# Down-projection pieces in the idle row groups of score phases, and shifted keys copied chunk by chunk

## Chip, cores, metric

One core of one Trainium2 chip runs the whole program. The metric is device time in microseconds, where smaller is better; most runs of one kernel agree within 0.1%. Kernels sent together ran on one chip, with runs of the kernel before in between.

## The reference, cut to what matters

A layer norm feeds two branches. One is attention with 32 heads of 16 channels that share one key and one value head. The other is a SiLU network of width 1792. All inputs are bf16, 2048 rows of 512.

```python
xn = layernorm(x)
s = attention(xn, wq, wk, wv, wo)     # 32 heads, Dh = 16, one k and one v for all
h = silu(xn @ w1)                     # (2048, 1792)
g = silu(h @ w2)                      # the "down projection"
return x + s * g
```

## The kernel before

The program is written by a planner that runs on the host: it simulates the five engines with fixed durations and, whenever an engine is free, places its next operation. What the chip gets is a fixed order for each engine and the semaphore waits between them. Four kinds of TensorE work alternate. A **score phase** computes three or four score tiles of 128 keys by 512 queries at once. Each tile has a contraction of only 32 rows (16 of them hold a head's channels), so it takes one of the array's four row groups and one bank of PSUM, the memory that TensorE writes its results to.

```python
def s_mm(pe, b, g, i, kt):     # tile of head group g, row group i, key block kt
    return pe.matmul(bank(b), lhsT=kt_sb[32 * i:32 * i + 32, g % 2, kt * P:(kt + 1) * P],
                     rhs=qt_sb[32 * i:32 * i + 32, (g // 2) % NQR, :],
                     start=True, stop=True, tile_position=(32 * i, 0))
```

A **column round** is four matmuls with all 128 contraction rows, each making 32 output rows of one bank. The value products are such rounds, and so are the rounds of the projection jobs. A down-projection job has 14 of them; the planner keeps one such job open at a time.

```python
def col4(h, b, lhs, rhs, start, stop, n=NQ):
    for j in range(4):
        last = h.matmul(bank(b)[32 * j:32 * (j + 1), 0:n], lhsT=lhs(j), rhs=rhs, start=start, stop=stop,
                        tile_position=(0, 32 * j), skip_group_check=True)
    return last
...
# mk_z, round ft of 14:
col4(pe, b, lambda j: u_sb[:, ft, r * P + 32 * j:r * P + 32 * (j + 1)], w2_sb[:, ft, :], ft == 0, ft == NFT - 1)
```

The exponential of a score tile is done in one of two ways: by ScalarE (one value product each), or by VectorE as an integer trick with three shifted copies made on GpSimd (four value products each). The odd head groups need the keys shifted down by 16 rows. These were zero-filled early and copied by four DMAs once all keys existed:

```python
pl.add(Task(PO, 1800.0, lambda g: g.memset(kt_sb[:, 1, :], 0.0), (), [("kt1", i) for i in range(4)], 3, ...))
...
def add_kt1():                 # called when the last of four key chunks is done
    for i in range(4):
        kt1[i] = pl.add(Task(SP, 60.0, lambda e, i=i: e.dma_start(
            kt_sb[32 * i + DH:32 * i + 32, 1, :], kt_sb[32 * i:32 * i + DH, 0, :]), ...
```

Thresholds in the planner are varied at random from a seed.

The softmax here doesn't subtract the row's maximum and nothing guards it: scores larger than these inputs give would overflow.

## Time and profile before

| | before |
|---|---|
| time, median of 4 (range) | 679.01 us (677.96 to 679.11) |
| profiled span | 677.3 us |
| busy: TensorE, ScalarE, VectorE, GpSimd | 98, 97, 90, 83% |
| score tiles, of these on VectorE | 2048, 732 |
| score phases of three and of four tiles | 536, 110 |
| column rounds of down-projection jobs | 224 |

A group line of the profile reads: source line, engine, operation, output and inputs by name, shapes, count, then busy time in us and mean ns of one, then the engine's idle time just before. The phases and rounds were counted by sorting TensorE's records in time. The lines themselves are in the prediction.

### The profile page before, as it was taken

How to read it: one execution, taken by the hardware profiler on the slowest of the kernel's cores; microseconds unless marked ns; L12 is line 12 of the kernel's file. 1: busy time of each engine (PE TensorE's matmuls, PEld its weight loads, DVE VectorE, ACT ScalarE, POOL GpSimd, SP SyncE). 2: the span in 40 equal slices, each digit the busy share in tenths (PEclk: the TensorE clock that was granted, in tenths of full speed). 3: DMA queues.
4: the chain of work that ended last, by engine and by line, in shares of the span. 5: the costliest groups of instructions: out<-in, count | busy, mean ns of one | idle time of the engine just before them, and what ended most of it. 6: DMA issues, size and time to landing. Idle time of an engine off the chain costs nothing.

```text
span 677.3 us, 21172 instructions
## 1 busy us (share of the span) xinstructions
PE 663.9 (98%) x8941; PEld 192.1 (28%) x8941; DVE 610.0 (90%) x1081; ACT 655.1 (97%) x763; POOL 564.9 (83%) x561
## 2 busy tenths in 40 slices
PE   7899999999999999999999999999999999999997
PEld 4322222222222222222222222222222222222233
DVE  8979998989889999998899999988989999998873
ACT  6899999999999999999999999999999999999995
POOL 3049888999998899899899889889989988998992
PEclk9989999999999999999999999999999999999999
DMA  8410000000000000000000010000000001000000
GB/s 302 137 18 1 3 2 2 2 2 2 2 2 17 19 17 17 2 2 2 2 1 2 3 33 17 18 2 1 2 2 2 2 1 33 18 18 2 2 1 33
DMA packets 11437, 12.66 MB, mean 19 GB/s; under 512 B 1808, under 2 KB 10768, under 8 KB 11344
## 3 DMA queue, kind: packets, MB, share of 16 engines
q1 hardware_dynamic: 11056, 11.05, 5.1%
q8 instruction: 72, 1.18, 0.7%
q10 hardware_dynamic: 288, 0.26, 0.1%
q14 instruction: 21, 0.17, 0.1%
HBM read 8.95 MB, written 2.10 MB: 16 GB/s over the span
## 4 chain that ended last, share of the span: by engine, by line
PE 76%; ACT 12%; DVE 9%; issue 1%; DMA 0%; ACTq 0%
PE ps L1177 32%; PE ps L847 26%; PE ps L503 18%; ACT pa_sb L1518 11%; DVE db_sb L1039 3%; DVE stats_sb L450 1%; DVE u_sb L652 1%; ACT t_sb L650 1%; DVE xn_sb L479 0%; DVE xnT_sb L530 0%; DVE f_sb L1224 0%; DMA ds_sb<-in_A_x_dram 0%; DVE fin_sb L702 0%; DVE otr_sb L1228 0%; DVE kt_sb L559 0%
## 5 line engine op out<-in xcount | busy, mean ns | idle before, releaser
L1106 POOL INT64_ADD ds_sb<-db_sb x549 | 559.2, 1040 | 98.5 <-DVE db_sb L1039 43.1
L1518 ACT ACTIVATE pa_sb<-ps 128x1024 bf16<-128x1024 f32 (+2 forms) x674 | 621.4, 1019 | 8.9 <-PE ps L847 7.9
L1039 DVE TENSOR_SCALAR db_sb<-ps 128x512 uint16<-128x512 f32 x732 | 474.9, 683 | 47.3 <-PE ps L847 40.6
L1177 PE MATMUL ps<-ds_sb,v_sb 128*32 128x512 bf16 x2196 | 274.9, 383 | 0.0
L847 PE MATMUL ps<-qt_sb,kt_sb 32*128 32x512 bf16 x2048 | 253.5, 385 | 5.9 <-ACT pa_sb L1518 1.8
L1177 PE MATMUL ps<-pa_sb,v_sb 128*32 128x512 bf16 x1316 | 243.7, 384 | 0.0
L1177 PE MATMUL ps<-db_sb,v_sb 128*32 128x512 bf16 x732 | 178.4, 384 | 0.6 <-DVE f_sb L1224 0.6
L847 PEld LDWEIGHTS ps<-qt_sb,kt_sb 32*128 32x128 bf16 x2048 | 63.1, 91 | 281.3 <-ACT pa_sb L1518 155.7
L1177 PEld LDWEIGHTS ps<-ds_sb,v_sb 128*32 128x32 bf16 x2196 | 68.5, 95 | 60.0 <-issue 41.2
L503 PE MATMUL ps<-xnT_sb,w_sb 128*32 128x512 bf16 x896 | 72.9, 386 | 0.0
L1177 PEld LDWEIGHTS ps<-pa_sb,v_sb 128*32 128x32 bf16 x1316 | 60.0, 95 | 38.9 <-issue 27.4
L503 PE MATMUL ps<-w_sb,u_sb 128*32 128x512 bf16 x896 | 70.7, 384 | 0.0
L1177 PEld LDWEIGHTS ps<-db_sb,v_sb 128*32 128x32 bf16 x732 | 43.8, 95 | 18.3 <-issue 12.5
L650 ACT ACTIVATE t_sb<-ps 128x512 bf16<-128x512 f32 x72 | 44.1, 613 | 0.0
L652 DVE SCALAR_TENSOR_TENSOR u_sb<-t_sb,ps 128x512 bf16<-128x512 bf16 x56 | 38.3, 684 | 0.8
L503 PEld LDWEIGHTS ps<-w_sb,u_sb 128*32 128x32 bf16 x896 | 17.2, 94 | 27.2 <-issue 23.1
L503 PEld LDWEIGHTS ps<-xnT_sb,w_sb 128*32 128x32 bf16 x896 | 16.7, 94 | 27.4 <-issue 22.0
L1224 DVE STREAM_TRANSPOSE f_sb<-ps 128x512 f32<-128x512 f32 x31 | 21.9, 706 | 0.0
L652 DVE SCALAR_TENSOR_TENSOR tmp_sb<-t_sb,ps 128x512 bf16<-128x512 bf16 x16 | 11.0, 685 | 10.0 <-ACT t_sb L650 9.6
L503 PE MATMUL ps<-xnT_sb,wq_sb 128*32 128x512 bf16 x240 | 19.5, 384 | 0.0
L503 PE MATMUL ps<-wo_sb,on_sb 128*32 128x512 bf16 x256 | 19.4, 383 | 0.0
L1228 DVE TENSOR_TENSOR otr_sb<-f_sb,rcp_sb 128x256 bf16<-128x256 f32 x31 | 12.9, 416 | 0.1
(67 smaller groups left out, 142.8 us busy)
## 6 DMA issues: line engine op xcount, KB each, us to landing
w_sb<-in_B_w_dram SPq DMA_DIRECT2D x2, 1792.0 KB, 12.8
xr_sb<-in_A_x_dram SPq DMA_DIRECT2D x16, 128.0 KB, 2.3
out_dram<-ob_sb SPq DMA_DIRECT2D x16, 128.0 KB, 1.7
ds_sb<-in_A_x_dram SPq DMA_DIRECT2D x3, 512.0 KB, 7.5
wq_sb<-in_A_wq_dram SPq DMA_DIRECT2D x1, 512.0 KB, 5.6
wo_sb<-in_A_wo_dram SPq DMA_DIRECT2D x1, 512.0 KB, 14.8
ds_sb<-in_A_x_dram SPq DMA_DIRECT2D x2, 128.0 KB, 2.7
ds_sb<-in_A_x_dram ACTq DMA_DIRECT2D x2, 128.0 KB, 2.9
```

The costliest lines, as they stand in the source:

```text
L450: ts_ = pl.add(Task(DV, 593.0, lambda v, t=t: v.bn_stats(stats_sb[:, t, :], x_tile(t)), [xkey(t)], [("st", t)], 1 + j, gate=(lambda j=j: S ...
L503: last = h.matmul(bank(b)[32 * j:32 * (j + 1), 0:n], lhsT=lhs(j), rhs=rhs, start=start, stop=stop, tile_position=(0, 32 * j), skip_group_c ...
L650: t1 = Task(AC, 490.0, lambda a: a.activation(t_sb[:, k, :], src, ACT.Tanh, scale=scale), [held], [("t", k)], 0, [t0])
L652: t2 = Task(DV, T_P, lambda v: v.scalar_tensor_tensor(out=dst, in0=t_sb[:, k, :], scalar=1.0, in1=src, op0=ALU.add, op1=ALU.mult), [held, ...
L847: return pe.matmul(bank(b), lhsT=kt_sb[32 * i:32 * i + 32, g % 2, kt * P:(kt + 1) * P], rhs=qt_sb[32 * i:32 * i + 32, (g // 2) % NQR, :], ...
L1039: bt.P[i] = pl.add(Task(DV, T_P, lambda v, b=b, i=i, bb=bt.b: v.tensor_scalar(db_sb[:, bb, i * NQ:(i + 1) * NQ], bank(b), 128.0 * LOG2E, 1 ...
L1106: whole["po"].append(pl.add(Task(PO, T_P64, lambda g, cols=cols: g.int64_add(ds_sb[:, s, cols].bitcast(U64), db_sb[:, bt.b, cols].bitcast( ...
L1177: h = pe.matmul(bank(OB)[32 * i:32 * (i + 1), :], lhsT=lhs, rhs=rhs, start=s0, stop=s1, tile_position=(0, 32 * i), skip_group_check=True)
L1224: t1 = pl.add(Task(DV, T_TR, lambda v: v.transpose(f_sb[:, k, :], bank(OB)), [("ps", OB)], [("F", k)], 1, [norm.get(("m", g - 2))]))
L1228: t3 = pl.add(Task(DV, 332.0, lambda v: v.tensor_tensor(o3[:, :, val:val + DH], f3[:, :, val:val + DH], rcp_sb[:, k, :].unsqueeze(2).to_br ...
L1518: op = pl.place(AC, 0.8333 * NQ * n + T_AF, lambda a: a.activation(pa_sb[:, s * NQ:(s + n) * NQ].rearrange("p (b n) -> p b n", n=NQ), ps3[ ...
```

## The change

The intent is to save TensorE time. In a phase of three tiles one row group idles. If a down-projection job is open, that row group now computes 32 rows of its contraction into the job's bank. Four such pieces, one in each row group, replace one column round. Three more things change with it. The shifted keys are copied chunk by chunk, by DMAs issued from ScalarE, so the odd head groups need not wait for the last chunk; the zero fill covers 16 rows instead of 128 and comes later. Eight seeds, one for each 64 phases, replace one seed. Three limits of the planner move (`PRESS_Z`, `START_Z`, `EARLY`; what they do is told before experiment 8).

```diff
+            def piece(ft, i, last):
+                rows, b = slice(32 * i, 32 * i + 32), jb.bank
+                return (lambda pe: pe.matmul(bank(b), lhsT=u_sb[rows, ft, r * P:(r + 1) * P], rhs=w2_sb[rows, ft, :],
+                                             start=False, stop=last, tile_position=(32 * i, 0), skip_group_check=True),
+                        ["w2", ("u", ft)])
...
+            if n == 3 and pl.mode != "S":
+                for jb in active:
+                    if jb.piece is not None and jb.pos > 0 and (jb.got or jb.end - 1 - jb.pos >= PIECE_MIN):
+                        pj = jb
...
+            if pj is not None and gap not in seen:
+                pj.got.add(gap)
+                if len(pj.got) == 4:
+                    pj.left -= 1
+                extra, rd = pj.piece(pj.end - 1, gap, pj.left == 0)
...
-        def add_kt1():
-            for i in range(4):
-                kt1[i] = pl.add(Task(SP, 60.0, ...
+        def add_kt1(c):
+            cols = slice(4 * c * P, 4 * (c + 1) * P)
+            kt1[c] = pl.add(Task(AC, T_ISSUE, lambda e: e.dma_start(kt_sb[DH:P, 1, cols], kt_sb[0:P - DH, 0, cols]),
...
-        pl.add(Task(PO, 1800.0, lambda g: g.memset(kt_sb[:, 1, :], 0.0), (), [("kt1", i) for i in range(4)], 3,
+        pl.add(Task(PO, 1800.0, lambda g: g.memset(kt_sb[0:DH, 1, :], 0.0), [("xn", 3)], [("kt1", c) for c in range(NC)], 3,
...
-SEED, SPREAD = 17, 0.1
+SEEDS, STRETCH, SPREAD = (1020, 3123, 1104, 3421, 7220, 2660, 1802, 97), 64, 0.1
+PIECE_MIN = 4
-PRESS_Z, PRESS_H = 18, 16
+PRESS_Z, PRESS_H = 20, 16
-START_Z, START_H = 6, 8
+START_Z, START_H = 4, 8
-WIDE, NMIN, EARLY = 3, 3, 200.0
+WIDE, NMIN, EARLY = 3, 3, 300.0
```

Cut here: the picking of tiles, which may now take an odd group as soon as its chunk's shifted keys are there, the bookkeeping of open jobs, and the planner's own estimate of when a small copy lands.

More of the change, by code (lines that the diff above doesn't have):

```diff
@@ L159, in place @@
         elif dma:
-            start = max(t0 + 1400.0, self.dma_t)
-            self.dma_t = start + dma / 250.0
-            op.vis = self.dma_t + 600.0
+            start = max(t0 + 1400.0, self.dma_t if dma > 1 else 0.0)
+            if dma > 1:
+                self.dma_t = start + dma / 250.0
+            op.vis = start + dma / 250.0 + 600.0
         self.clk[eng] = op.end
@@ L374, in bass_recurrent_scan__grouped_kv_mqa__dense_activation_silu__prompt_kernel @@
         pl = Planner()
-        rng = Random(SEED)
+        rng = [Random(SEEDS[0])] if SEEDS else []
         def vary(x):
-            return x * (1.0 + SPREAD * (rng.random() - 0.5)) if SEED else x
+            return x * (1.0 + SPREAD * (rng[-1].random() - 0.5)) if rng else x
         outs = []
@@ L495, in job @@
             jb.preds, jb.bank, jb.fixed, jb.mode, jb.gate = preds, bk, bk is not None, mode, gate
-            jb.pos, jb.done = 0, False
+            jb.pos, jb.end, jb.got, jb.left, jb.piece, jb.prev = 0, len(rounds), set(), len(rounds), None, None
             jb.tasks = {}
@@ L684, in mk @@
                 def mk(b):
+                    last = jb.left == 1
                     return lambda pe: col4(pe, b, lambda j: u_sb[:, ft, r * P + 32 * j:r * P + 32 * (j + 1)],
-                                           w2_sb[:, ft, :], ft == 0, ft == NFT - 1)
+                                           w2_sb[:, ft, :], ft == 0, last)
                 return mk
+            def piece(ft, i, last):
[3 more added lines that the diff above has]
+                        ["w2", ("u", ft)])
             def consume(jb, op):
@@ L694, in consume @@
                 return tmp_task[tt].first
-            job("z", tt, pace, [(rnd(ft), ["w2", ("u", ft)], MM) for ft in range(NFT)], consume,
+            jb = job("z", tt, pace, [(rnd(ft), ["w2", ("u", ft)], MM) for ft in range(NFT)], consume,
                 gate=lambda: all((c, ft) in u_task and u_task[c, ft].op is not None for ft in range(NFT))
                 and (tt < 8 or tt - 8 in fin_task and fin_task[tt - 8].op is not None))
+            jb.piece = piece
         def scaled(tt, b):
@@ L835, in slot_ok @@
                 return False
-            if g % 2 and (i not in kt1 or kt1[i].op is None):
+            if g % 2 and (kt // 4 not in kt1 or kt1[kt // 4].op is None):
                 return False
@@ L839, in slot_ok, with slot_time @@
             return oi in q_done and q_done[oi].op is not None
+        def slot_time(g, i):
+            return pl.ready(PE, s_reads(g, i, left[g, i][0]), ()) if slot_ok(g, i) else None
         def s_reads(g, i, kt):
             k = [("qT", (g // 2) % NQR)]
-            k.append(("kt0", kt) if g % 2 == 0 else ("kt1", i))
+            k.append(("kt0", kt) if g % 2 == 0 else ("kt1", kt // 4))
             return k
@@ L884, in d_batch, with pick_a @@
             return bt
-        def pick_a(n, avoid):
+        def pick_a(n, avoid, t):
             res = []
@@ L899, in pick_a @@
                             if len(res) < n and a_left(gg, i) > 0 and (i not in used or not strict and not res):
-                                if not slot_ok(gg, i):
-                                    return None if not res else res
+                                st_ = slot_time(gg, i)
+                                if st_ is None or st_ > t + 30:
+                                    continue
                                 res.append((gg, i, take(gg, i)))
@@ L904, in pick_a @@
                                 again = True
-            return res
+            return res or None
         class Unit:
@@ L916, in s_phase_ready @@
                 return None
-            if not all(slot_ok(g, i) for i in range(4) if left[g, i]):
+            when = None
+            for gg in (g, g + 1):
+                if gg >= NG or not any(a_left(gg, i) > 0 for i in range(4)):
+                    continue
+                ts = [slot_time(gg, i) for i in range(4) if left[gg, i]]
+                if None in ts:
+                    continue
+                if when is None or max(ts) < when and when > pl.clk[PE] + 30:
+                    when = max(ts)
+            if when is None:
                 return None
@@ L929, in s_phase_ready @@
                 return None
-            i = next(i for i in range(4) if left[g, i])
-            st["n"] = n
-            r = max(bt[n - 1][0], pl.ready(PE, s_reads(g, i, left[g, i][0]), ()))
+            r = max(bt[n - 1][0], when)
             if n < 4:
@@ L968, in do_S @@
                     want = 1
+            pj = None
+            if n == 3 and pl.mode != "S":
+                for jb in active:
+                    if jb.piece is not None and jb.pos > 0 and (jb.got or jb.end - 1 - jb.pos >= PIECE_MIN):
+                        pj = jb
+                if pj is not None:
+                    gap = min((i for i in range(4) if i not in pj.got), key=lambda i: (sum(len(left[gg, i]) for gg in range(st["gA"], min(st["gA"] + 2, NG))), i))
+                    avoid.add(gap)
             want = min(want, 2 if bl < two else 1 if bl < one else 0)
@@ L973, in do_S @@
                     break
-                need = [i for i in range(4) if i not in bt.slots and i not in avoid and left[bt.g, i] and slot_ok(bt.g, i)]
+                need = [i for i in range(4) if i not in bt.slots and i not in avoid and left[bt.g, i] and slot_ok(bt.g, i) and slot_time(bt.g, i) <= t + 30]
                 if not need:
@@ L986, in do_S @@
             st["la"] = n - nd
-            sl = pick_a(min(n - nd, 3), avoid)
+            sl = pick_a(min(n - nd, 3), avoid, t)
             if sl is None:
@@ L1016, in do_S @@
                 seen[i] = seen.get(i, 0) + 1
+            extra = None
+            if pj is not None and gap not in seen:
[3 more added lines that the diff above has]
+                extra, rd = pj.piece(pj.end - 1, gap, pj.left == 0)
+                reads += rd
+                writes.append(("ps", pj.bank))
+                seen[gap] = 1
+                st["pieces"] = st.get("pieces", 0) + 1
             dur = MM * max(seen.values())
@@ L1022, in emit @@
                     h = s_mm(pe, b, g, i, kt)
-                return h
-            op = pl.place(PE, dur, emit, sorted(set(reads)), writes, t0=max(t, pe_start(pl.clk[PE], "S")))
+                if extra is not None:
+                    h = extra(pe)
+                return h
+            op = pl.place(PE, dur, emit, sorted(set(reads), key=str), writes, t0=max(t, pe_start(pl.clk[PE], "S")),
+                          after=pj.prev if extra is not None else None)
+            if extra is not None:
+                pj.prev = op
             pl.set_mode("S")
+            if extra is not None and len(pj.got) == 4:
+                pj.got = set()
+                pj.end -= 1
+                finish(pj, op)
+            st["phases"] = st.get("phases", 0) + 1
+            if st["phases"] % STRETCH == 0 and len(SEEDS) > len(rng):
+                rng.append(Random(SEEDS[len(rng)]))
             for b, sl_ in zip(abanks, sl):
@@ L1241, in bass_recurrent_scan__grouped_kv_mqa__dense_activation_silu__prompt_kernel @@
         kt1 = {}
-        def add_kt1():
-            for i in range(4):
-                kt1[i] = pl.add(Task(SP, 60.0, lambda e, i=i: e.dma_start(
-                    kt_sb[32 * i + DH:32 * i + 32, 1, :], kt_sb[32 * i:32 * i + DH, 0, :]),
-                    [("kt0", k) for k in range(NKT)], [("kt1", i)], 0, list(evac_kt.values()), dma=64 * 1024))
+        def add_kt1(c):
+            cols = slice(4 * c * P, 4 * (c + 1) * P)
+            kt1[c] = pl.add(Task(AC, T_ISSUE, lambda e: e.dma_start(kt_sb[DH:P, 1, cols], kt_sb[0:P - DH, 0, cols]),
+                                 [("kt0", k) for k in range(4 * c, 4 * c + 4)], [("kt1", c)], -1,
+                                 [evac_kt[4 * c], evac_kt[4 * c + 3]], dma=1))
         def progress():
@@ L1294, in job_round @@
             for jb in active:
-                if jb.pos >= len(jb.rounds):
+                if jb.pos >= jb.end - (1 if jb.got else 0):
                     continue
@@ L1310, in do_job, with finish @@
             jb.pos += 1
+            jb.left -= 1
             if jb.kind == "T":
                 t_done.update(jb.arg)
-            if jb.kind == "w" and jb.pos == len(jb.rounds):
+            if jb.kind == "w" and jb.left == 0:
                 w_rounds.add(jb.arg)
-            if jb.pos == len(jb.rounds):
+            finish(jb, op)
+        def finish(jb, op):
+            if jb.left == 0:
                 tasks = jb.consume(jb, op)
@@ L1327, in do_job @@
                     pl.add(tk)
-                if jb.kind == "K" and jb.arg == NC - 1:
-                    add_kt1()
+                if jb.kind == "K" and all(k in evac_kt for k in range(4 * jb.arg, 4 * jb.arg + 4)):
+                    add_kt1(jb.arg)
         pass
```

## The prediction

> **What bounds the kernel now.** I read the page's busy shares first, then a table of busy time by stretch, then the waits, the groups with their shapes, and last the timeline of TensorE in one down-projection job and of ScalarE at the start. The busy shares and slices:
>
> ```profile
> PE 663.9 (98%) x8941; PEld 192.1 (28%) x8941; DVE 610.0 (90%) x1081; ACT 655.1 (97%) x763; POOL 564.9 (83%) x561
> ...
> PE   7899999999999999999999999999999999999997
> ...
> ACT  6899999999999999999999999999999999999995
> POOL 3049888999998899899899889889989988998992
> ```
>
> Two engines are full at once, TensorE and ScalarE; both are slack only in the first slices and the last one. The stretches say it more sharply (columns: stretch, its length, then busy us with instruction counts of PE, PEld, DVE, ACT and POOL, then clock, DMA share, GB/s):
>
> ```profile
> 12.00:20.00 8.00, 7.10 (x137) 3.87 (x135) 7.72 (x26) 6.99 (x7) 0.00 (x0) 1.00 1.06 383
> 20.00:30.00 10.00, 7.81 (x113) 3.39 (x114) 9.52 (x34) 8.02 (x14) 0.00 (x0) 1.00 0.36 118
> 30.00:40.00 10.00, 8.59 (x121) 3.42 (x117) 7.52 (x17) 9.83 (x16) 0.00 (x0) 0.98 0.13 22
> ...
> 260.00:360.00 100.00, 99.91 (x1341) 27.34 (x1338) 92.09 (x151) 99.42 (x113) 91.71 (x91) 1.00 0.01 2
> ```
>
> From 60 to 660 us TensorE is busy over 99.5% and ScalarE 98.5 to 99.7% of each stretch, VectorE 91 to 93%, GpSimd 88 to 92%. The largest waits in the view of waits, those of the score phases' weight loads on the exponential (155.7 us) and on VectorE's eviction (102.7 us), are loads waiting for a PSUM bank behind a matmul stream that has no gap, so they cost nothing. The groups give the exchange rate between the two full engines:
>
> ```profile
> L1518 ACT ACTIVATE pa_sb<-ps 128x1024 bf16<-128x1024 f32 x630 | 595.6, 1038 | 7.4 <-PE ps L847 6.4
> L1039 DVE TENSOR_SCALAR db_sb<-ps 128x512 uint16<-128x512 f32 x732 | 474.9, 683 | 47.3 <-PE ps L847 40.6
> ```
>
> Of the 2048 score tiles, ScalarE exponentiates 1316 at 621.4/1316 = 0.472 us each; 732 go to VectorE's four-shift form, which takes four value products instead of one. So moving one tile from ScalarE to VectorE frees 0.472 us of ScalarE and costs TensorE three more matmuls, 3/4 of a round of four.
>
> **What the Trainium skill says.** (1) "TensorE: Matmul & The Clock Gate", Part 3 on packing small matmuls: matmuls in different row groups run at the same time, the span being one matmul plus about 4 ns for each further tile. The trace agrees: I sorted TensorE's records in time into score phases and rounds and took the medians from one's start to the next one's. A phase of three takes 0.321 us up to the following column round (525 of them), one of four 0.325 us (109 of them): a fourth row group costs 4 ns. (2) "TensorEngine Tiling (Array Packing)", Key Properties: changing the tiling mode drains the engine. Agrees: column round to column round is 0.226 us at the median (mean 0.221), column round to phase 0.322 us, so each switch costs some 0.1 us. (3) The same page, Gotcha 1: different row tiles must write different PSUM banks at one time. The pieces obey it: three score banks and the job's own. (4) "DMA: Bandwidth & Descriptors", queues, rings and completion order: an engine of the DMA takes turns between the queue rows at packet granularity, so a small copy issued from ScalarE need not wait behind the weights on SyncE's queue. No run here yet shows it for such a copy; the four key copies of before, made when the queues were quiet, took 2.9 us to land.
>
> **The change, part by part.**
>
> Pieces. There are 646 score phases, 536 of three tiles and 110 of four (536x3 + 110x4 = 2048). In a phase of three the idle row group now gets 32 rows of a down-projection contraction; four such pieces replace one column round of four matmuls. What matters is how many three-wide phases fall inside a down-projection job once it has started, because only those carry pieces. One job of before on TensorE:
>
> ```profile
> 289.48 0.39 PE L503 MATMUL ps<-w_sb,u_sb 128*32 128x512 bf16 x4
> 289.80 0.39 PE L847 MATMUL ps<-qt_sb,kt_sb 32*128 32x512 bf16 x3
> 290.12 0.62 PE L503 MATMUL ps<-w_sb,u_sb 128*32 128x512 bf16 x8
> 290.67 0.39 PE L847 MATMUL ps<-qt_sb,kt_sb 32*128 32x512 bf16 x3
> ```
>
> The job's 14 rounds are over in 5.8 us with six phases among them. Over the 16 jobs I count 129 phases between first and last round, all of them three wide, for jobs lasting 4.5 to 15.4 us. A set of pieces is only begun while at least four more rounds remain besides it, and the last round goes first; walking this rule along the 16 sequences gives one set for 13 jobs and two for three, 19 rounds replaced by 76 pieces, out of 224. The promise of 129/4 = 32 is thus not reached. Removed: 19 x 0.221 = 4.2 us; added: 76 x 0.004 = 0.3 us. Matmuls stay the same in number; z's column matmuls fall from 896 to some 820, and some 76 of 32 rows appear. TensorE gains 3.9 us, no more than 0.6% of its span. No phase and no mode switch goes away by it.
>
> That gain can only be had if ScalarE gets shorter too. If ScalarE and TensorE stay balanced and x tiles move, ScalarE falls by 0.472x and TensorE by 3.9 - 0.75 x 0.221x = 3.9 - 0.166x. Equal at x = 6.1, worth 2.9 us. Six tiles more are under 1% of VectorE's and GpSimd's load, which have 8 to 10% free.
>
> Shifted keys by chunk. Odd groups need keys shifted by 16 rows. Before, these came after the last of four key chunks, at 36.8 us; now each chunk has its own copy of 112 rows and the odd group can be scored with it. This helps at the start, where ScalarE runs dry between chunks:
>
> ```profile
> 12.00 5.48 ACT L1518 ACTIVATE pa_sb<-ps 128x1536 bf16<-128x1536 f32 x4
> 17.97 1.51 ACT L1518 ACTIVATE pa_sb<-ps 128x1024 bf16<-128x1024 f32 x2 [0.49 <-PE ps L847]
> 20.93 3.03 ACT L1518 ACTIVATE pa_sb<-ps 128x1024 bf16<-128x1024 f32 x4 [1.44 <-PE ps L847]
> 23.84 0.60 ACT L650 ACTIVATE t_sb<-ps 128x512 bf16<-128x512 f32 x1
> 24.32 4.58 ACT L1518 ACTIVATE pa_sb<-ps 128x512 bf16<-128x512 f32 x8
> 29.95 8.35 ACT L1518 ACTIVATE pa_sb<-ps 128x512 bf16<-128x512 f32 x13 [1.05 <-PE ps L847]
> ```
>
> The bracketed idle times to 41 us add up to 3.4 us (0.49, 1.44, 1.05, and 0.16 and 0.24 after these lines). The 21 one-wide exponentials cost about 0.58 us each (4.58/8 = 0.57, 8.35/13 = 0.64 with gaps inside) against 0.472, another 2.3 us. So 5.7 us could be won at most. TensorE has as much to give: gaps of 4.1 us between 13 and 39 us, and 17 rounds of clock-keeping filler. Against it stands that the four issues are moved onto ScalarE, where the two input loads' issues took 0.90 us together: 4 x 0.45 = 1.8 us. Leaves 3.9 us; not all one-wide work becomes two-wide while VectorE is busy with the layer norm to 36 us (no tile goes to VectorE until all keys exist), so I take 2.2 us.
>
> Seeds and thresholds. The schedule is random in its thresholds; now the seed is chosen anew every 64 phases instead of once. A phase costs 0.322 us and its way in 0.1 us, so ten phases fewer of 646 (three-wide joined to four-wide) are worth 4.2 us of TensorE. I can't derive the number; 2.0 us is a judgement, about 5 phases. The pieces pull the other way, since they need three-wide phases.
>
> Sum: 679.0 - 2.9 - 2.2 - 2.0 = 671.9; I say 672.0.
>
> **Rivals.** (a) ScalarE is the bound and TensorE's gain turns into idle time: the 99.4% busy ScalarE speaks for it, the planner's choice of tiles by ScalarE's backlog against it. Then only the start and the seeds count: about 675. (b) A new wait: the first chunk's copy would be issued at some 12 us, when the DMA engines are full (share 1.06, with weight loads taking 12.8 us to land). If it lands 5 us later than planned, TensorE, which keeps its order, stops and ScalarE behind it; the two gains at the start are gone and some 2 us more: about 676. The taking of turns speaks against it. (c) The jobs linger: with a higher pressure limit and a lower start limit, down-projection jobs could span 10 phases each, giving 40 replaced rounds, 8.8 us of TensorE, 6.5 us in all; with luck in the seeds about 665. The uninterrupted jobs of before (ten of them with six phases or fewer) speak against it.
>
> **Range and chances.** The sum's parts are each uncertain by 2 to 3 us, so 666 to 677 should hold it 8 times in 10. Two per cent faster is under 665.4, which needs (c) or a lucky schedule: 0.10. Slower by 2% would need a stall of over 20 us: 0.03. Within 2%: 0.87.
>
> **What would show it.** Right: 70 to 100 new 32-row matmuls with the down-projection weights, in phases that still take about 0.325 us; column rounds of those jobs down by a quarter as many; tiles on VectorE up from 732 by 5 to 15; TensorE and ScalarE both still over 99% between 60 and 660 us; ScalarE's idle time from 12 to 41 us cut from 3.4 us to under 2 us, with four issues of 0.45 us each on it; copies landing in 2 to 4 us. Wrong: ScalarE full with TensorE under 98.5% in the middle (a); a gap of over 2 us before a score phase of an odd group before 25 us (b); more than 130 pieces (c); a phase count below 635, which would mean that the seeds did more than the pieces.

## The result, and the profile after

The changed kernel took 672.18 us (median of 4, 672.11 to 672.25) against 679.01 us, with a correct result. The ratio is 0.9903, 95% interval 0.9886 to 0.992. Ratios here are the mean time of one kernel's fast runs over that of the other's of the same rounds, so not quite the ratio of the medians.

The page after, by engine and by the groups that the change touches:

```profile
PE 658.4 (98%) x8958; PEld 191.4 (29%) x8958; DVE 608.6 (91%) x1085; ACT 651.5 (97%) x756; POOL 566.7 (85%) x564
...
L1090 DVE TENSOR_SCALAR db_sb<-ps 128x512 uint16<-128x512 f32 x736 | 474.4, 682 | 38.8 <-PE ps L860 27.5
...
L505 PE MATMUL ps<-w_sb,u_sb 128*32 128x512 bf16 x816 | 64.2, 384 | 0.0
...
L694 PE MATMUL ps<-w_sb,u_sb 32*128 32x512 bf16 x80 | 30.8, 385 | 0.0
```

There are 80 pieces, and the job's column matmuls fall from 896 to 816, which is 20 rounds. The phases went from 646 to 642, and the tiles on VectorE from 732 to 736. The timeline of TensorE in a job after:

```profile
102.83 0.60 PE L505 MATMUL ps<-w_sb,u_sb 128*32 128x512 bf16 x8
103.47 0.39 PE L860 MATMUL ps<-qt_sb,kt_sb 32*128 32x512 bf16 x3
103.48 0.38 PE L694 MATMUL ps<-w_sb,u_sb 32*128 32x512 bf16 x1
103.80 0.62 PE L505 MATMUL ps<-w_sb,u_sb 128*32 128x512 bf16 x8
```

The piece starts 10 ns after the phase's start and the next round 0.33 us after it; in the lines of before in the prediction, without a piece, it is 0.32 us. Busy time by stretch after (same columns as in the prediction):

```profile
12.00:20.00 8.00, 6.78 (x138) 3.97 (x135) 7.72 (x27) 6.95 (x8) 0.00 (x0) 1.00 1.06 377
20.00:30.00 10.00, 9.08 (x137) 3.88 (x137) 9.52 (x34) 9.35 (x14) 0.00 (x0) 1.00 0.51 160
...
260.00:360.00 100.00, 99.84 (x1355) 27.48 (x1359) 92.33 (x153) 99.30 (x113) 92.53 (x92) 1.00 0.01 2
```

The middle looks as before; the start is fuller from 20 us on. Following the count of scored tiles shows where the 6.8 us arose. The phase that brings it to 16 starts 1.6 us earlier than before (18.9 against 20.5 us), to 64, 2.3 us earlier (41.0 against 43.3), to 256, 3.8 us (102.3 against 106.1), to 1024, 5.0 us (337.2 against 342.2) and to 2048, 6.1 us (659.4 against 665.5). So about a third comes in the first 41 us and the rest along the way.

Two things in the start were not in my prediction. The **clock** of TensorE, the third figure from the end in these lines of the stretches of before, was halved for 3.4 us near 40 us:

```profile
36.00:38.00 2.00, 1.01 (x24) 0.59 (x20) 1.41 (x3) 2.00 (x4) 0.00 (x0) 1.00 0.00 0
38.00:40.00 2.00, 1.91 (x22) 0.44 (x22) 2.00 (x4) 1.84 (x4) 0.00 (x0) 0.90 0.63 107
40.00:42.00 2.00, 2.00 (x18) 0.35 (x14) 0.86 (x2) 1.76 (x4) 1.74 (x2) 0.50 0.20 33
42.00:44.00 2.00, 2.00 (x27) 0.63 (x27) 1.51 (x3) 1.61 (x4) 1.33 (x2) 0.75 0.00 0
```

In the changed kernel the same stretch has the full clock:

```profile
40.00:42.00 2.00, 1.74 (x24) 0.44 (x21) 1.79 (x4) 2.00 (x4) 1.79 (x2) 1.00 0.00 0
```

And the **first exponential** began at 11.47 instead of 12.00 us. The timelines of VectorE and GpSimd before suggest why:

```profile
5.52 0.80 DVE L467 TENSOR_SCALAR var_sb<-mv_sb 128x2 f32<-128x2 f32 x1
```

```profile
4.49 1.81 POOL L427 MEMSET kt_sb<- 128x2048 bf16 x1
```

VectorE's operation on two columns took 0.80 us and ended at 6.32 us, when GpSimd's zero fill ended (6.30 us). After the change the fill comes later and the same operation is short:

```profile
5.61 0.15 DVE L469 TENSOR_SCALAR var_sb<-mv_sb 128x2 f32<-128x2 f32 x1
```

### The profile page after: what moved, and what is told of

Read it like the earlier page. It is cut to its first block, busy times and chain, and to the rows that moved or that the text cites. A ratio compares the mean times of both kernels' runs of the same rounds, so it can differ in the third digit from the quotient of the medians.

```text
span 670.4 us, 21190 instructions
## 1 busy us (share of the span) xinstructions
PE 658.4 (98%) x8958; PEld 191.4 (29%) x8958; DVE 608.6 (91%) x1085; ACT 651.5 (97%) x756; POOL 566.7 (85%) x564
## 4 chain that ended last, share of the span: by engine, by line
PE 78%; ACT 12%; DVE 8%; issue 1%; DMA 0%; ACTq 0%; DVEq 0%
PE ps L1228 34%; PE ps L860 26%; PE ps L505 18%; ACT pa_sb L1572 11%; DVE db_sb L1090 3%; DVE stats_sb L452 1%; ACT t_sb L652 1%; DVE u_sb L654 1%; DMA ds_sb<-in_A_x_dram 0%; DVE xnT_sb L532 0%; DVE xn_sb L481 0%; DVE fin_sb L712 0%; DVE f_sb L1275 0%; DVE mv_sb L456 0%; DVE kt_sb L561 0%
## 5 line engine op out<-in xcount | busy, mean ns | idle before, releaser
L1228 PE MATMUL ps<-ds_sb,v_sb 128*32 128x512 bf16 x2208 | 265.9, 383 | 0.0
L1228 PE MATMUL ps<-db_sb,v_sb 128*32 128x512 bf16 x736 | 165.0, 384 | 0.3 <-DVE f_sb L1275 0.3
L1228 PEld LDWEIGHTS ps<-ds_sb,v_sb 128*32 128x32 bf16 x2208 | 65.6, 95 | 62.8 <-issue 46.1
L505 PE MATMUL ps<-w_sb,u_sb 128*32 128x512 bf16 x816 | 64.2, 384 | 0.0
L1228 PEld LDWEIGHTS ps<-db_sb,v_sb 128*32 128x32 bf16 x736 | 40.9, 95 | 21.5 <-issue 14.5
L694 PE MATMUL ps<-w_sb,u_sb 32*128 32x512 bf16 x80 | 30.8, 385 | 0.0
L505 PEld LDWEIGHTS ps<-w_sb,u_sb 128*32 128x32 bf16 x816 | 15.6, 95 | 22.3 <-issue 18.5
L505 PE MATMUL ps<-xnT_sb,wq_sb 128*32 128x512 bf16 x240 | 18.9, 384 | 0.0
```

Source lines behind the costliest of these rows:

```text
L694: return (lambda pe: pe.matmul(bank(b), lhsT=u_sb[rows, ft, r * P:(r + 1) * P], rhs=w2_sb[rows, ft, :], start=False, stop=last, tile_posit ...
L1228: h = pe.matmul(bank(OB)[32 * i:32 * (i + 1), :], lhsT=lhs, rhs=rhs, start=s0, stop=s1, tile_position=(0, 32 * i), skip_group_check=True)
```

## The experiments

Twelve kernels ran. All gave correct results. The planner re-plans everything when an input changes and the seed alone moves the outcome, so each edit either keeps the order of instructions (called "schedule kept") or uses a seed chosen for its planned length: from the middle of 40 seeds; in the fourth, as long as the plan of before; in the last, the best plan found.

### 1. Putting the replaced rounds back (schedule kept)

```diff
                 if extra is not None:
                     h = extra(pe)
+                if back is not None:      # set at every fourth piece
+                    h = col4(pe, back, lambda j: zer_sb[:, 32 * j:32 * (j + 1)], zer_sb[:, :], False, False)
```

> The changed kernel with its schedule kept instruction for instruction, except that after every fourth piece TensorE also runs one column round of four matmuls with zero weights into the same bank: the 20 rounds that the pieces replaced are put back, and nothing else. Theory (TensorE is on the path all the time, so its rounds are the gain): 20 x 0.221 = 4.4 us longer, 676.6 us, and ScalarE's idle time between 60 and 650 us grows by about as much. Rival (TensorE had slack there and ScalarE is the bound): under 1 us longer.

Measured: 676.42 us (676.40 to 676.52), 4.2 us longer than the changed kernel. The 20 rounds were expected to take 4.4 us, so TensorE time is on the path nearly one for one. My expectation on ScalarE's idle time was wrong: between 46 and 640 us it grew only from 4.2 to 6.1 us, though the kernel became 4.2 us longer. That is a first hint that ScalarE's share of busy time hides something (see below).

### 2. The zero fill alone (schedule kept)

```diff
-... g.memset(kt_sb[:, 1, :], 0.0), (), [("kt1", i) for i in range(4)], 3,
+... g.memset(kt_sb[:, 1, :], 0.0), [("xn", 3)], [("kt1", i) for i in range(4)], 3,
```

> The kernel before with one edit: the zero fill of the shifted keys on GpSimd waits for the fourth normalised tile, as in the change; keys still come late and by four copies. Theory: in the kernel before this fill (4.5 to 6.3 us) held up a tiny VectorE operation of the layer norm, which took 0.80 us where the same one takes 0.15 us in the changed kernel; moving it alone starts the first exponential about 0.5 us earlier, as in the changed kernel (11.5 us against 12.0), and the time falls by about 0.5 us. Rival (the earlier start of the changed kernel was a faster landing of the first inputs): no change in the first exponential, within 0.1 us of 12.0.

Measured: 677.26, 677.57, 678.56 and 678.61 us. The runs of before in the same call fall into two groups as well: one at 677.76 and six from 678.73 to 679.01. Each group of the experiment is about 0.4 us below the matching one. The tiny operation took 0.15 us:

```profile
5.54 0.15 DVE L467 TENSOR_SCALAR var_sb<-mv_sb 128x2 f32<-128x2 f32 x1
```

The first exponential began by 11.4 us. The theory holds; by this comparison of matching groups the fill cost about 0.4 us. The ratio (0.9989, 0.9974 to 1.0004) alone would not have shown it, because of the two groups.

### 3. Filler where TensorE was thin (schedule kept)

```diff
 # value round of the last key chunk, before its own matmuls
+for _ in range(2 if c == NC - 1 else 0):
+    pe.matmul(bank(b)[:, 128:512], lhsT=zer_sb[:, 0:P], rhs=zer_sb[:, 128:512], start=True, stop=True)
```

> The kernel before, its schedule kept, with two zero matmuls of 384 columns put ahead of each of the two value rounds of the last key chunk, in stretches where TensorE was idle (36 to 38 us). Theory: the half clock that the kernel before was granted for 3.4 us from 39.6 us followed from the thin TensorE work just before; with filler the clock stays at 1.0 and the time falls by 1.2 to 1.7 us (half of 3.4 us). Rival (the dip belongs to the run or to something else): the dip stays and the time rises by 0 to 0.5 us.

Measured: 677.98 us, all runs between 677.80 and 678.05, and the full granted clock over the whole profiled run:

```profile
36.00:38.00 2.00, 1.64 (x28) 0.96 (x24) 1.43 (x3) 2.00 (x4) 0.00 (x0) 1.00 0.00 0
40.00:42.00 2.00, 1.96 (x26) 0.48 (x23) 1.54 (x4) 2.00 (x5) 1.76 (x2) 1.00 0.20 33
```

The gain over the median of before is 1.0 us, a little under what I expected. More telling is that the two groups of before (677.8 and 679.0) have shrunk to the lower one, in all four runs, while six of the seven runs of before were in the upper one. So filler at this place keeps the half clock away, and the half clock costs 1.2 us in the runs that have it. How thin the work must be does not come out: TensorE was busy for 2.33 of the 3.41 us before the dip (36.17 to 39.58 us), but in experiment 7 it was busy for 2.25 of 3.41 us (11.61 to 15.02 us) and the clock stayed full. That it strikes only some runs fits what the Trainium skill says in "TensorE: Matmul & The Clock Gate", Part 1: activity is judged in free-running windows of 3413 ns. Here the dip lasted 3413 ns exactly, and the full clock before it 34.13 us (5.45 to 39.58 us), ten times as long; no run sets the phase of the window on purpose, so that part stays an inference.

### 4. The keys by chunk, without pieces

```diff
-SEEDS, STRETCH, SPREAD = (1020, 3123, 1104, 3421, 7220, 2660, 1802, 97), 64, 0.1
-PIECE_MIN = 4
+SEEDS, STRETCH, SPREAD = (33,), 64, 0.1
+PIECE_MIN = 99        # and START_Z 6, PRESS_Z 18, EARLY 200.0, as before
```

> The changed kernel without pieces, with the old limits of before and one seed chosen so that the planner's own schedule is as long as that of before: what remains of the change is the shifted keys by chunk, issued on ScalarE, and the later zero fill. Theory: the start is ahead of before by 2.0 to 2.5 us at the 64th score tile, as in the changed kernel, no half clock near 40 us, and the whole kernel is 2 to 3 us faster, 676 to 677 us. Rival (the lead is given back, since the issues cost ScalarE 2.2 us and the later work is the same): within 0.5 us of before.

Measured: 676.25 us (676.17 to 676.35), 2.7 us below before, with the 64th tile at 41.0 us as in the changed kernel and no half clock near 40 us. Against the runs of before that had the full clock (677.8 us) it is 1.5 us; the zero fill is some 0.4 us of that. So the 2.7 us are about 0.4 for the fill, 1.2 for the clock, and a remainder of 1.1. This takes the parts to add up; no run has the keys by chunk without the later fill. The clock stayed up with TensorE busy for 1.46 us from 36 to 38 us, where it was 1.01 us in before; that odd-group work fills this stretch is the plan's intent and not visible in the trace. The remainder is not all the keys' either. At the 64th tile experiment 4 leads before by 2.3 us, experiment 3 (filler) by 1.3 and experiment 2 (fill) by 0.5, so only some 0.5 us of the lead at that point is left for the keys; the rest comes later, where the plan and its seed differ too.

### 5 and 6. No pieces, two ordinary seeds

```diff
-SEEDS, STRETCH, SPREAD = (1020, 3123, 1104, 3421, 7220, 2660, 1802, 97), 64, 0.1
-PIECE_MIN = 4
+SEEDS, STRETCH, SPREAD = (18,), 64, 0.1     # 14 in the other
+PIECE_MIN = 99
```

> The changed kernel without pieces, with one seed in place of eight; seed 18, whose planned schedule is the middle of 40 seeds for this variant, so that luck of the seed is left out. Theory (pieces are worth 0.74 of the TensorE time they free, since tiles move to VectorE): against the one-seed kernel with pieces, 2.5 to 4 us slower, about 676 to 677 us; about four fewer tiles on VectorE than with pieces. Rival (the gain of the change is the seeds and the limits): within 1 us of the one-seed kernel with pieces.

> The same with another seed from the middle of its 40, seed 14: it shows how much a seed alone moves the time. Expected within 1 us of the other kernel without pieces.

Measured: 676.26 and 676.15 us. With pieces and an ordinary seed (experiment 7) it is 673.17 us, so pieces are worth 3.0 to 3.1 us. But the tiles on VectorE were 736 and 732 without pieces and 736 with them: none need move. Where the time went shows at the end of TensorE's timeline without pieces, seed 18:

```profile
661.81 0.61 PE L1228 MATMUL ps<-pa_sb,v_sb 128*32 128x512 bf16 x8
662.24 3.19 PE L505 MATMUL ps<-w_sb,u_sb 128*32 128x512 bf16 x56
665.26 3.63 PE L505 MATMUL ps<-wo_sb,on_sb 128*32 128x512 bf16 x64
```

and with pieces (experiment 7):

```profile
661.95 0.60 PE L1228 MATMUL ps<-ds_sb,v_sb 128*32 128x512 bf16 x4
662.34 0.39 PE L1228 MATMUL ps<-pa_sb,v_sb 128*32 128x512 bf16 x1
662.37 3.60 PE L505 MATMUL ps<-wo_sb,on_sb 128*32 128x512 bf16 x60
```

Both score their last tile at 660 us. Without pieces a whole down-projection job of 14 rounds (56 matmuls, 3.2 us) is left over after the last value round, ahead of the output projection.

### 7. One ordinary seed for the eight

```diff
-SEEDS, STRETCH, SPREAD = (1020, 3123, 1104, 3421, 7220, 2660, 1802, 97), 64, 0.1
+SEEDS, STRETCH, SPREAD = (28,), 64, 0.1
```

> The changed kernel with one seed, 28, from the middle of 40 seeds for this variant, in place of the eight seeds. Theory (the eight seeds are worth about 1 us over an ordinary single seed): 673 to 673.7 us. Rival (the eight seeds are a large part of the gain): 675 us or more.

Measured: 673.17 us (673.10 to 673.31), 1.0 us above the changed kernel, as the theory had it.

### 8. The old limits, with pieces

```diff
+SEEDS, STRETCH, SPREAD = (32,), 64, 0.1
-PRESS_Z, PRESS_H = 20, 16
+PRESS_Z, PRESS_H = 18, 16
-START_Z, START_H = 4, 8
+START_Z, START_H = 6, 8
-WIDE, NMIN, EARLY = 3, 3, 300.0
+WIDE, NMIN, EARLY = 3, 3, 200.0
```

> The changed kernel with pieces, but with the old limits (a down-projection job starts at a pressure up to 6 instead of 4, value rounds push it aside from 18 instead of 20, phases of fewer than four tiles come 200 instead of 300 ns early) and one seed, 32, from the middle of its 40. Theory (the limits are worth something because jobs run more in one piece and phases are fewer): 1.5 to 3 us slower than the one-seed kernel with the new limits. Rival (they are worth nothing): within 0.7 us of it.

Measured: 676.04 us, 2.9 us above experiment 7. The limits matter about as much as the pieces, at ordinary seeds. Phases differ by one only (643 against 642), so my reason, fewer phases, is not what does it; where the time goes, and which of the three limits does it, was not tried. This kernel must not be set against experiment 4, whose seed was a lucky one.

### 9 and 10. Pieces in one half of the jobs

```diff
-            jb.piece = piece
+            jb.piece = piece if tt < 8 else None      # seed 31; in the other tt >= 8, seed 32
```

> The changed kernel with one ordinary seed and pieces only in the first eight down-projection jobs. The two theories: my prediction's (freed TensorE time is turned into tiles moved from ScalarE to VectorE, anywhere in the kernel) lets half the pieces earn half, so about 674.7 us, between the one-seed kernel with all pieces (673.2) and those with none (676.2). The theory formed after the runs without pieces (score phases end at 660 us with and without pieces, at 736 tiles on VectorE both times; the gain is that no down-projection job is left over after the last value round): a job left over costs some 3 us whole or nothing, so either about 673.5 or about 676 us, with the 14 rounds visible after the last value round or not.

> The same with pieces only in the last eight jobs. First theory: about 674.7 us as well. Second theory: these pieces are used just where jobs lag at the end, so closer to all pieces, 673.2 to 674.5 us, without a left-over job.

Measured: 674.86 us with 40 pieces in the first half and 674.04 us with 36 in the last. In the first, a job of 14 rounds is again left over after the last score, yet the last score comes 1.3 us earlier than with all pieces (658.8 against 660.1 us). In the second none is left over and the last score comes 1.2 us later (661.3). The theory of a left-over job that costs all or nothing falls: half the rounds earn 1.3 to 2.2 of the 3.0 us. What holds in all these runs is only the sum of TensorE's work: its busy time orders these kernels nearly as their times do (experiment 7: 658.5 us busy, time 673.17; 10: 660.6, 674.04; 9: 661.0, 674.86; 5: 662.4, 676.26; 6: 663.0, 676.15). Where a shortage of it shows, in a left-over job or in later scores, is the planner's choice.

### 11. Pieces in the up-projection jobs too

```diff
+PMIN = {"z": 4, "h": 2, "q": 99, "w": 99}
-... (jb.got or jb.end - 1 - jb.pos >= PIECE_MIN)
+... (jb.got or jb.end - 1 - jb.pos >= PMIN[jb.kind])
 # mk_h: a piece as in mk_z, from w1_sb and xnT_sb; seed 10. Two more kinds of job, q and w, get one too,
 # but the limit 99 keeps them from ever using it
```

> The changed kernel with one seed and pieces also in the 56 up-projection jobs of four rounds (a set is begun after the first round), correct results. Theory (TensorE rounds are the gain): 16 or more rounds fewer, 3 us faster than the one-seed kernel, 670 us. Rival (a job of four rounds has to stay open over at least four phases, holding a PSUM bank and the one job place, so phases narrow or jobs lag): slower than it by 1 to 3 us, 674 to 676 us.

Measured: 675.85 us, 2.7 us slower than experiment 7, although 88 pieces replaced 22 rounds of the up-projection. The down-projection had 76 pieces here against 80 there, so 21 rounds fewer in all:

```profile
L506 PE MATMUL ps<-xnT_sb,w_sb 128*32 128x512 bf16 x808 | 65.2, 383 | 0.4 <-DVE u_sb L664 0.3
L686 PE MATMUL ps<-xnT_sb,w_sb 32*128 32x512 bf16 x88 | 33.8, 384 | 0.0
```

The rival is right in its result. TensorE's idle time between 46 and 640 us grew from 2.3 to 6.6 us, and the tiles on VectorE fell to 724. That the open job's bank or its place is to blame was argued and not tried apart, and this variant was planned anew with a seed of its own.

### 12. Other seeds and one other limit

```diff
-SEEDS, STRETCH, SPREAD = (1020, 3123, 1104, 3421, 7220, 2660, 1802, 97), 64, 0.1
+SEEDS, STRETCH, SPREAD = (1742, 9433), 64, 0.1
-HOLD, Q_LEAD = 1000.0, 3.3
+HOLD, Q_LEAD = 1200.0, 3.3
```

> The changed kernel with two other seeds and value rounds held back for up to 1.2 instead of 1.0 us, the best of some thousands of planned schedules: an attempt at a version that beats both. Expected 0.5 to 1 us faster than the changed kernel, 671.2 to 671.7 us; rival: within 0.3 us of it.

Measured: 671.82 us (671.71 to 672.03) against 672.18 us; the ratios to before are 0.9912 (0.9897 to 0.9927) and 0.9903 (0.9886 to 0.992). They were run at other times. This is no version that surely beats the changed one. In this call most runs of before were at 677.8 us instead of 679.0 us, which is why a lower time has the higher ratio.

## Why the prediction was right, and where not

The time, 672.18 us, is 0.2 us from the 672.0 predicted. Of the 6.8 us gained, 2.7 go with the changes at the start (experiment 4, in a plan of its own) and 3.0 to the pieces (experiments 5 to 7). That leaves 1.1 for seeds and limits. The terms were 2.2, 2.9 and 2.0. Each is less certain than its sum, since the seeds differ and the parts need not add up. That the sum came within 0.2 us is partly luck: of the three terms only the pieces had the right size, and that by a step that did not happen.

**Pieces: the count was right.** It said 19 rounds and 76 pieces; there were 20 and 80. (Counted again, nine jobs of before and not ten have six phases or fewer, and the last has only three, too few for a set, so the rule gives 18.) A phase with a piece took 0.325 us at the median (79 of them), as the four-tile phases of before promised; the extra row group costs the 4 ns of the prediction.

**Pieces: the step from TensorE time to kernel time failed, though its number held.** The step of the prediction read "If ScalarE and TensorE stay balanced and x tiles move ... Equal at x = 6.1, worth 2.9 us". The worth was 3.0 to 3.1 us, but no tile moved between kernels with and without pieces at 736. With the order kept, the rounds were worth 4.2 of 4.4 us, so TensorE's time went into the kernel's almost whole, with no second engine sharing it. The error was reading ScalarE as full. Its 1024-wide exponentials last at least 1017 ns each but can follow one another every 904 ns. I took all 585 of these between 60 and 640 us in the records of before and measured from each one's start to the next operation's start. The least is 904 ns and the mean 935 ns, so 585 x 31 ns = 18 us of waiting, while the profile's idle time for the engine from 46 to 640 us is 4.2 us. Waits shorter than the overlap of 113 ns vanish in a share of busy time. 443 of the 585 intervals are within 17 ns of the least; the other 142 hold 16 of the 18 us. The changed kernel has the same mean (934 ns). Experiment 1 bears this out: over all 637 of these exponentials, the time beyond 904 ns from start to start grew from 23.4 us in the changed kernel to 27.2 us, 3.8 of the 4.2 us, while the visible idle time grew by 1.9. No run made ScalarE's own work longer, so how much longer it could have been at no cost is not shown. The re-planned kernels gave 3.0 instead of 4.2 us because the planner arranged them otherwise; how that 1.2 us divides was not settled.

**Keys: the mechanism was partly right and its size made up of other parts.** ScalarE's idle time from 12 to 41 us fell from 3.4 to 2.0 us (1.05, 0.44, 0.20 and 0.34), at the edge of what I expected, with 0.61 and three times 0.52 us of issues on it, 2.2 us where I had 1.8. But an issue is not always a cost: the first and third ran while an exponential was under way, and the next one followed without a gap; only at the second and fourth was ScalarE idle, for 0.44 and 0.34 us. The 2.3 us for narrow exponentials were misread too. A merged line of the timeline shows the shape of its first operation: of the 21, five were two tiles wide, and the one-wide ones followed each other every 0.48 us where nothing held them up, against 0.45 us a tile in the two-wide ones. The keys were worth at most about 1.1 us (experiment 4). The other 1.6 us of the start were the zero fill (0.4) and the clock (1.2). Neither was in the working, though the view of before's stretches that I had read showed a clock of 0.85 from 40 to 50 us. I passed over it as a trifle.

**Seeds and limits** were the judgement of the working: 2.0 against about 1.1. Eight seeds instead of an ordinary one gained 1.0 us and the limits 2.9 us at ordinary seeds, while before had the best plan among 40 seeds (its planner, run on the host for seeds 1 to 40, plans 671.2 us for its seed 17, the shortest, and 672.9 in the middle), so most of that was owed already. The step "about 5 phases" was close in number, four fewer (642), but not in cause: one ordinary seed has 642 phases as well (experiment 7).

**Rivals.** (a), ScalarE as the bound, is excluded by experiment 1. (b), a stall on a late copy, did not come: landing took 2.2 to 6.6 us (median 4.2), above the 2 to 4 us expected, but the view of waits from 12 to 40 us has no wait on that copy. The first two, issued while weights were loading, took 6.6 and 6.3 us, the last two 2.2 us each. The taking of turns, point (4) of the prediction, did show: the first copy was issued 2.0 us after the second load of `w_sb` and landed 6.4 us before it. (c), lingering jobs, did not come: 12 jobs had one set of pieces and four had two. Of my signs, "tiles on VectorE up by 5 to 15" was wrong (4), and ScalarE was below 99% in two of six stretches (98.8 and 98.5%).

## What to carry to other kernels

Put work into idle row groups when a second stream of long accumulations is open anyway: each piece cost 4 ns here, but the variant that also kept jobs of four rounds open to collect pieces was 2.7 us slower, for a reason not tried apart. Before calling an engine full, compare the least and the mean time from start to start of its main operation, for a share of busy time hides waits shorter than the overlap of consecutive operations. And read the clock of every stretch of the start: thin TensorE work at one point was paid for here with 1.2 us, in a stretch of 3.4 us at half clock.

## What the Trainium skill lacked or had wrong

- "TensorE: Matmul & The Clock Gate", Part 1, has the free-running window and that runs differ by it while the clock warms up; what it lacks is that one thin stretch in the middle of a tuned program makes its runs fall into two groups. Here these were 677.8 and 679.0 us, and two zero matmuls ahead of each of two value rounds left only the lower group (677.80 to 678.05).
- "SBUF — State Buffer", Who interferes with whom, says that VectorE in a two-port mode contends with GpSimd and that the one that issues second blocks fully. The case fits, and shows that it holds down to an operation on only 128x2 float32 elements: 0.80 us beside a zero fill of 1.81 us, 0.15 us without it.
- "ScalarE: Activation LUTs", What ACT_TABLE_LOAD costs, says that back-to-back activations overlap by about 93 ns. Here 1024-wide exponentials from PSUM overlapped by 113 ns (1017 against 904 ns), and no page warns that a busy share then hides shorter waits: 18 us of waiting in the kernel before, where the idle time shows 4.2.
- "DMA: Bandwidth & Descriptors" has no landing time for a small copy inside SBUF beside a bulk load: 112 rows of 1 KB took 6.6 and 6.3 us from issue to landing while weights were loading (issued at 11.6 and 19.9 us), and 2.2 us each afterwards.
